# VectorE's program moved to a block border, and the first piece of wo loaded in eight parts by partitions, in a gated mix of cached attention and a feed-forward block

## The chip, the cores and the metric

The kernel runs on one core of a Trainium2 chip. The metric is device time in microseconds (us) of one execution, the median of several runs; lower is better. A core has the engines PE (TensorE: matrix products, with its weight loads as PEld), DVE (VectorE), ACT (ScalarE), POOL (GpSimd) and SP (SyncE, which here only issues DMA transfers), and 16 DMA engines that carry out the transfers between the chip's memory (HBM) and the core's memory (SBUF, 128 partitions, each a row of bytes). [...] The engines run independently and wait for each other on semaphores.

## What is computed

One token is decoded. Two branches, attention over a cache and a gated feed-forward block, are mixed by a gate:

```python
def _A_ref(x, k_cache, v_cache, wq, wo):      # Hq 32, Hkv 8, Sk 32768, Dh 128, D 512
    q = (x @ wq).reshape(B, Sq, Hq, Dh).transpose(0, 2, 1, 3)
    k = jnp.repeat(k_cache, 4, axis=1)
    v = jnp.repeat(v_cache, 4, axis=1)
    scores = jnp.einsum("bhqd,bhkd->bhqk", q, k) * (Dh ** -0.5)
    o = jnp.einsum("bhqk,bhkd->bhqd", _softmax(scores), v)
    return o.transpose(0, 2, 1, 3).reshape(B, Sq, Hq * Dh) @ wo

def _B_ref(x, w1, w3, w2):                    # F 1792
    return (_silu(x @ w1) * (x @ w3)) @ w2

g = _sigmoid((x * gate_w).sum(-1, keepdims=True))
return g * a + (1 - g) * b
```

All is float32. Keys and values are 8 heads x 32768 positions x 128 each, 134 MB apiece; wq and wo are 8.4 MB each, and w1, w3 and w2 are 3.7 MB each.

## The kernel before

The kernel is written as a list of operations for each engine (class `Program`, L24 to L115). `pr.add` records an operation with the names of what it reads and writes, and works out which semaphores it must wait for; `emit` writes each engine's list in the order in which it was recorded. So the order in the source is the order on each engine. `load` (L195) records a DMA issue on SP for a tile and takes one of nine semaphores in turn; `over` names tiles whose readers must be done first. TensorE's loops over the key units and value units are hardware loops (L701, L707); the other engines' lists are unrolled, with about 250 instructions on VectorE.

SBUF holds two buffers, `big_a` and `big_b`, each of 128 partitions x 64 KB. The keys come in 16 units and the values in 16 units, each 128 x 64 KB (8.4 MB), into one or the other buffer. A unit of keys is set aside in part by ScalarE, transposed by VectorE in blocks (L366), and multiplied with the queries by TensorE (L350). After four units come the softmax (L400 to L424) and, lagging by four units, the values' products (L451). So one unit is in the transfer queues behind the other nearly all the time, and SP issues the next as soon as its buffer's last reader is done.

At the end stand: four last units of values (`load_unit`, L589), `w2` (L604), and then `wo` (L607 to L610) into `big_a`, as `wo_t` with 32 slices of 512 numbers to a partition. It is loaded in six pieces of 16, 7, 4, 2, 2 and 1 slices (`parts`), all with 128 rows: the piece of 16 slices has 32 KB a partition. Each piece may be issued once the products of the unit that lay in `big_a` are done. TensorE multiplies with the first three pieces in `wide` (L626, its matmuls at L630), one call to a piece, each waiting for that piece's load; VectorE adds the sum to `acc` (L652), and `ff_down` (L657, L661) multiplies with the last three pieces as they come in. A copy (L673) and two stores of two rows each (SP and ScalarE, L504) end the kernel. `tile_critical` at L156 opens the part that is written by hand; ahead of it lies the opening barrier of all engines.

Of the kernel before, what the change touches and what calls it, by code (L numbers as in the profile page):

```python
# [13 lines left out]
P = 128  # L14
# [104 lines left out]
def kernel(  # L119
# [13 lines left out]
    nc = tc.nc  # L133
# [18 lines left out]
    FJ = F // 4  # L152
    assert DH == P and D == 4 * P and REP == 4 and HKV == 8 and F == FR * P and S == 4 * P * NB

    critical = ctx.enter_context(ExitStack())
    critical.enter_context(tc.tile_critical(sync_engine=mybir.EngineType.Activation, no_gpsimd_drain=True))  # L156
    pr = Program(nc, tc.alloc_semaphore)
# [12 lines left out]
    wo_t = big[0].rearrange("p (k e) -> p k e", k=32)  # L170
# [15 lines left out]
    otp = kt[1][:, 0:1024].rearrange("p (k c) -> p k c", c=32)  # L186
# [8 lines left out]
    def load(dst, src, writes, over=()):  # L195
        lanes[0] += 1
        lane = f"load{lanes[0] % 9}"
        return pr.add(
            "SP", lambda: nc.sync.dma_start(dst, src), writes=writes, over=[*over, lane], inc=lane, by=16, also=lane,  # L199
        )  # L200
# [81 lines left out]
    for c in range(NC):  # L282
        def part(c=c):
# [18 lines left out]
         reads=["gate0"], writes=["gate1"])  # L302
# [39 lines left out]
    def window(t, z):  # L342
        return act(
            lambda: A.copy(winc, win[:, t // 4, :, 16 - 16 * z:48 - 16 * z]),  # L344
            reads=[("win", t // 4, r) for r in range(4)], writes=["winc"], credit="windows",
        )
# [162 lines left out]
    first = window(0, 0)  # L509
    for t in range(NH):  # L510
# [9 lines left out]
        if t + 1 < NH:  # L520
            load_keys(t + 1)
            first = window(t + 1, 0)
# [83 lines left out]
        values(7, 0, z, region(0, z), f"A{z}")  # L606
    wod = wo.rearrange("(p k) e -> p k e", k=32)  # L607
    parts = ((0, 16), (16, 23), (23, 27), (27, 29), (29, 31), (31, 32))
    for a, b in parts:
        load(wo_t[:, a:b, :], wod[:, a:b, :], [("wo", a)], over=["A0", "A1"])  # L610


# [13 lines left out]
    def wide(i, ws, **kw):  # L626
        def go():
            for j, (w, t) in enumerate(ws):
                r = 32 * (j % 4)
                ins = T.matmul(pa[r:r + 32, :], w, t, start=(i == 0 and j < 4), stop=(final[j % 4] == (i, j)))  # L630
            return ins
        pe(go, writes=["f0"], **kw)


    def down(ks):
# [9 lines left out]
        reads=[("each", 0), ("each", 1), "otp"], writes=["lay"])  # L645
# [2 lines left out]
    down(range(3, FR))  # L648
    laid = ["otp", "lay"]
    for i, (a, b) in enumerate(parts[:3]):  # L650
        wide(i, [(otp[:, k, :], wo_t[:, k, :]) for k in range(a, b)], reads=[*laid, ("wo", a)])
    dve(lambda: V.tensor_add(acc, acc, pa), reads=["acc", "f0"], writes=["acc"])  # L652


# [27 lines left out]
    a, b, c, d = flips  # L682
# [67 lines left out]
```

## Time and profile before

| | |
|---|---|
| time, median of 3 runs | 693.98 us (693.81 to 694.11) |
| span of the profiled execution | 692.4 us |
| the profiled execution's own time beside its span | not given apart; the median lies 1.6 us above the span |
| mean granted TensorE clock | 0.790 |
| bytes read from HBM | 296.23 MB, 428 GB/s over the span |
| DMA queue q1 (SP's loads) | 6052 packets, 99.1% of 16 engines' span |
| packets of kind "instruction" | q8: 5 with 0.08 MB; q14: 3 with 0.02 MB |
| last load of wo issued, and its landing | 653.5 us, 688.5 us |

The page cuts the span into slices and gives the busy share of each engine, and for the DMA engines the mean share of the 16 and what they moved. "Instruction" packets carry program code to the engines; all other packets here are data. The windows view gives, for a stretch of time, the busy time and instructions of PE, PEld, DVE, ACT and POOL in this order, and then TensorE's clock, the DMA share and GB/s. The issue of a load stands on the SP queue (SPq); its landing is told by the semaphore that it raises.

### The profile page before, as it was taken

Reading aid. Unit: us, or ns where it says so; the run is one execution under the profiler, and the core shown is the slowest. Engines: PE = TensorE matmul, PEld = TensorE weight load, DVE = VectorE, ACT = ScalarE, POOL = GpSimd, SP = SyncE. Lnnn points to the kernel's source line nnn. Section 1 sums busy time; section 2 is a strip of 40 time slices with the busy share of each in tenths; the row PEclk is TensorE's granted clock in tenths of the full one; section 3 lists DMA queues with packets and bytes.
Section 4 is the critical chain, followed back from the end, with each engine's and each line's share of the span. In section 5 each row is a group of like instructions: output and inputs, shape, how many; then the busy total and the mean of one; then the engine's idle time right before and its main releaser. Section 6 shows DMA issues by size and latency. Waiting matters only on the chain. (4 is left out here: it accounts for less than half of the span.)

```text
span 692.4 us, 5704 instructions
## 1 busy us (share of the span) xinstructions
PE 402.8 (58%) x2430; PEld 94.6 (14%) x2430; DVE 368.4 (53%) x229; ACT 134.6 (19%) x113; POOL 8.1 (1%) x34
## 2 busy tenths in 40 slices
PE   1537777566474656557484645666573646744575
PEld 0101111201010110201010101201010102211121
DVE  0049999394735637493726537593826546700026
ACT  0143223232303130220303131210303131100000
POOL 4000000000000000000000000000000000000000
PEclk9969999958667676977786777778586777776689
DMA  9999999999999999999999999999999999999996
GB/s 386 455 428 424 424 424 436 448 443 424 428 428 428 435 454 432 424 432 428 432 454 435 424 428 428 432 435 451 432 424 428 428 435 454 435 421 424 433 421 284
DMA packets 6068, 296.34 MB, mean 428 GB/s; under 512 B 678, under 2 KB 682, under 8 KB 1068
## 3 DMA queue, kind: packets, MB, share of 16 engines
q1 hardware_dynamic: 6052, 296.23, 99.1%
q8 instruction: 5, 0.08, 0.0%
q14 instruction: 3, 0.02, 0.0%
q10 hardware_dynamic: 8, 0.01, 0.0%
HBM read 296.23 MB, written 0.00 MB: 428 GB/s over the span
## 5 line engine op out<-in xcount | busy, mean ns | idle before, releaser
L366 DVE STREAM_TRANSPOSE aside<-big_a 128x2048 f32<-128x2048 f32 x41 | 94.3, 2300 | 166.9 <-DMA big_a<-in_A_k_cache_dram 166.9
L350 PE MATMUL ps<-aside,winc 128*32 128x512 f32 x512 | 96.0, 830 | 142.4 <-PEq L688 141.5
L350 PE MATMUL ps<-kt,winc 128*32 128x512 f32 x512 | 96.2, 832 | 61.2 <-PEq L688 61.2
L451 PE MATMUL ps<-big_b,pv 128*32 128x512 f32 x768 | 96.1, 657 | 17.5 <-PEq L688 17.5
L338 ACT COPY aside<-big_a 128x6144 f32<-128x6144 f32 x14 | 74.4, 5313 | 151.8 <-DMA big_a<-in_A_k_cache_dram 151.8
L366 DVE STREAM_TRANSPOSE kt<-aside 128x2048 f32<-128x2048 f32 x32 | 73.4, 2293 | 17.2 <-PE ps L350 17.2
L366 DVE STREAM_TRANSPOSE kt<-big_a 128x2048 f32<-128x2048 f32 x28 | 63.5, 2269 | 0.0
L379 ACT COPY sb<-ps 128x512 f32<-128x512 f32 x16 | 17.1, 1069 | 156.8 <-PE ps L350 156.8
L350 PEld LDWEIGHTS ps<-aside,winc 128*32 128x32 f32 x512 | 13.4, 125 | 215.7 <-issue 215.7
L451 PEld LDWEIGHTS ps<-big_b,pv 128*32 128x32 f32 x768 | 27.7, 120 | 88.1 <-issue 88.1
L366 DVE STREAM_TRANSPOSE aside<-aside 128x2048 f32<-128x2048 f32 x16 | 36.3, 2269 | 0.0
L583 DVE TENSOR_TENSOR sb<-ps,own_b 128x512 f32<-128x512 f32 x2 | 1.4, 691 | 60.8 <-PE ps L574 60.8
L350 PEld LDWEIGHTS ps<-kt,winc 128*32 128x32 f32 x512 | 13.3, 123 | 143.8 <-issue 143.8
L574 PE MATMUL ps<-big_b,probs 128*32 128x512 f32 x128 | 18.0, 726 | 18.8 <-DMA big_b<-in_A_v_cache_dram 18.8
L344 ACT COPY winc<-win 128x128 f32<-128x128 f32 x32 | 9.8, 306 | 78.7 <-PE ps L350 78.7
L574 PE MATMUL ps<-big_a,probs 128*32 128x512 f32 x128 | 17.3, 703 | 10.1 <-DMA big_a<-in_A_v_cache_dram 10.1
L614 PE MATMUL ps<-win,ones 128*128 128x512 f32 x42 | 22.7, 635 | 0.0
L366 DVE STREAM_TRANSPOSE aside<-big_b 128x2048 f32<-128x2048 f32 x7 | 16.0, 2291 | 11.4 <-DMA big_b<-in_A_k_cache_dram 11.4
L262 PE MATMUL ps<-acc 128*128 128x512 f32 x34 | 20.0, 670 | 2.5 <-POOL acc L219 1.6
L400 DVE TENSOR_REDUCE mt<-turned 128x8 f32<-128x2048 f32 x4 | 9.2, 2291 | 22.6 <-PE turned L389 22.6
L424 DVE TENSOR_REDUCE sums<-probs 128x8 f32<-128x2048 f32 x4 | 15.2, 3801 | 2.1 <-ACT probs L417 2.1
L288 PE MATMUL turned<-big_a,xp 128*32 128x512 f32 x64 | 8.5, 691 | 12.1 <-DMA big_a<-in_A_wq_dram 12.1
(93 smaller groups left out, 186.6 us busy)
## 6 DMA issues: line engine op xcount, KB each, us to landing
big_b<-in_B_w_dram SPq DMA_DIRECT2D x2, 3584.0 KB, 20.8
big_a<-in_A_wo_dram SPq DMA_DIRECT2D x1, 4096.0 KB, 27.6
aside<-in_B_w_dram SPq DMA_DIRECT2D x1, 3584.0 KB, 37.4
big_a<-in_A_wo_dram SPq DMA_DIRECT2D x1, 1792.0 KB, 31.5
big_a<-in_A_wo_dram SPq DMA_DIRECT2D x1, 1024.0 KB, 33.5
big_a<-in_A_wo_dram SPq DMA_DIRECT2D x2, 512.0 KB, 34.7
big_a<-in_A_wo_dram SPq DMA_DIRECT2D x1, 256.0 KB, 35.2
big_a<-in_A_k_cache_dram SPq DMA_DIRECT2D x14, 26.3
```

The costliest lines, as they stand in the source:

```text
L262: return T.matmul(ps_s, acc[:, 0:P], acc, start=True, stop=False, skip_group_check=True)
L288: ins = T.matmul(pf[b][32 * j:32 * j + 32, :], xp[:, c, :], t[:, o:o + REP * DH], start=(c == 0), stop=(c == NC - 1),)
L338: act(lambda: A.copy(spare, src[:, :, 32:128]), reads=[key], writes=["wo"])
L344: lambda: A.copy(winc, win[:, t // 4, :, 16 - 16 * z:48 - 16 * z]),
L350: ins = T.matmul(ps_s[32 * g:32 * g + 32, :], winc[:, c, :], kt[c % 2][:, 512 * g:512 * g + 512], start=False, stop=False, skip_group_chec ...
L366: k = dve(lambda d=dst, s=src: V.transpose(d, s), reads=[key], writes=[f"kt{c % 2}"], over=["kt0"] * (t >= LAG and (z, c) == (1, 1)), cred ...
L379: lambda: A.copy(sb[:, :, :, t % 4], ps_s.rearrange("p (n i) -> p n i", i=32)),
L400: dve(lambda: V.tensor_reduce(mt[:, 0:8], turned.rearrange("p (n q) -> p q n", q=8), axis=AX.X, op=ALU.max), reads=banks, writes=["mt"])
L424: dve(lambda: V.tensor_reduce(sums[:, 8 * w:8 * w + 8].rearrange("p (u q) -> p u q", u=2), probs[:, :, 0:1024].rearrange("p u (n q) -> p u ...
L451: ins = T.matmul(ps_o[32 * t:32 * t + 32, :], pv[:, o:o + 32], big[1][:, n * P:(n + 4) * P], start=((z, g) == (0, 0)), stop=((z, g) == (1, ...
L574: ins = T.matmul(ps_o[32 * t:32 * t + 32, :], prob[u][:, o:o + 32], vt[:, n * P:(n + 4) * P], start=((e, z, g) == (0, 0, 0)), stop=((e, z, ...
L614: return T.matmul(bank[:, 0:n], ones, win.rearrange("p w c n -> p (w c n)")[:, 0:n], start=True, stop=True)
```

## The change

The first edit is one instruction for VectorE alone, ahead of the hand-written part: `addr_align(128, offset=0, max_nops=0)` has the loader put what follows at the next multiple of 128 instructions in VectorE's program, and has it jumped to, not padded with no-ops.

The second is the first piece of wo, the one with 16 slices. It was one load of 128 rows with 32 KB each. It becomes: one load of the rows 112 to 127 with 13 of the 16 slices (26 KB a row), six loads of the last three slices of these rows (6 KB a row), three rows at a time and the last with one, and one load of the rows 0 to 111 with all 16 slices. The eight loads raise one common semaphore, `first`, and the first call of `wide` waits for all of them. The other five pieces are as before.

```diff
+    nc.vector.addr_align(128, offset=0, max_nops=0)
     critical = ctx.enter_context(ExitStack())
...
     parts = ((0, 16), (16, 23), (23, 27), (27, 29), (29, 31), (31, 32))
-    for a, b in parts:
+    top_rows, split = 112, 13
+    pieces = [(top_rows, P, 0, split)]
+    pieces += [(p, min(p + 3, P), split, 16) for p in range(top_rows, P, 3)]
+    pieces += [(0, top_rows, 0, 16)]
+    first = [("wo", 0, i) for i in range(len(pieces))]
+    for key, (p, q, a, b) in zip(first, pieces):
+        pr.add("SP", lambda p=p, q=q, a=a, b=b: nc.sync.dma_start(wo_t[p:q, a:b, :], wod[p:q, a:b, :]),
+               writes=[key], over=["A0", "A1"], inc="first", by=16)
+    for a, b in parts[1:]:
         load(wo_t[:, a:b, :], wod[:, a:b, :], [("wo", a)], over=["A0", "A1"])
...
     for i, (a, b) in enumerate(parts[:3]):
-        wide(i, [(otp[:, k, :], wo_t[:, k, :]) for k in range(a, b)], reads=[*laid, ("wo", a)])
+        landed_keys = [("wo", a)] if i else first
+        wide(i, [(otp[:, k, :], wo_t[:, k, :]) for k in range(a, b)], reads=[*laid, *landed_keys])
```

On SP, behind the last unit of values, the loads of w2 (`in_B_w`) and wo stood so before (destination, source, and the rows and numbers to a row of each):

```order
L199 DMA aside<-in_B_w_dram 128x7168
L199 DMA big_a<-in_A_wo_dram 128x8192
L199 DMA big_a<-in_A_wo_dram 128x3584
L199 DMA big_a<-in_A_wo_dram 128x2048
L199 DMA big_a<-in_A_wo_dram 128x1024 x2
L199 DMA big_a<-in_A_wo_dram 128x512
```

And so they stand now (the lines of the changed kernel are one or ten higher):

```order
L200 DMA aside<-in_B_w_dram 128x7168
L616 DMA big_a<-in_A_wo_dram 16x6656
L616 DMA big_a<-in_A_wo_dram 3x1536 x5
L616 DMA big_a<-in_A_wo_dram 1x1536
L616 DMA big_a<-in_A_wo_dram 112x8192
L200 DMA big_a<-in_A_wo_dram 128x3584
L200 DMA big_a<-in_A_wo_dram 128x2048
L200 DMA big_a<-in_A_wo_dram 128x1024 x2
L200 DMA big_a<-in_A_wo_dram 128x512
```

The load of 128 rows with 8192 numbers each has become eight; all others keep their place and shape.

At the start of VectorE's list, the branch that waits for the opening barrier was followed at once by the branch that waits for ScalarE's opening of the hand-written part:

```order
L745 UNCONDITIONAL_BRANCH [waits barrier_Pool_Activation_PE_DVE_SP_release]
L745 UNCONDITIONAL_BRANCH [waits Activation_sequencer_49]
L279 COPY xp<-ps 128x4 [waits PE]
L298 TENSOR_REDUCE gsm<-tmp 1x1 [waits POOL]
L309 STREAM_TRANSPOSE aside<-probs 128x512 [waits ACT]
```

Now the alignment stands between the two (the row "ISA"):

```order
L755 UNCONDITIONAL_BRANCH [waits barrier_Pool_Activation_PE_DVE_SP_release]
L155 ISA
L755 UNCONDITIONAL_BRANCH [waits Activation_sequencer_49]
L280 COPY xp<-ps 128x4 [waits PE]
L299 TENSOR_REDUCE gsm<-tmp 1x1 [waits POOL]
L310 STREAM_TRANSPOSE aside<-probs 128x512 [waits ACT]
```

No other engine has it, and VectorE's own operations keep their order.

## The prediction

> **What bounds the kernel now.** I read the page's slices first, then the queues, the chain of waits, and last the end of the span in narrow windows.
>
> ```profile
> span 692.4 us, 5704 instructions
> PE 402.8 (58%) x2430; PEld 94.6 (14%) x2430; DVE 368.4 (53%) x229; ACT 134.6 (19%) x113; POOL 8.1 (1%) x34
> DMA  9999999999999999999999999999999999999996
> DMA packets 6068, 296.34 MB, mean 428 GB/s; under 512 B 678, under 2 KB 682, under 8 KB 1068
> q1 hardware_dynamic: 6052, 296.23, 99.1%
> q8 instruction: 5, 0.08, 0.0%
> q14 instruction: 3, 0.02, 0.0%
> ```
>
> No engine is busy for 60% of the span, but the 16 DMA engines are at nine tenths in every slice but the last: q1, SP's loads, keeps them busy for 99.1%. So the kernel is its bytes. An engine at work moves 428 / (16 x 0.991) = 27.0 GB/s, that is 27.0 KB (of 1000 bytes) a microsecond. Two things may shift an end that is already full: bytes dealt unevenly to the 16 engines, and a lower rate. The last two rows matter for the first: eight packets of q8 and q14 fetch program code (0.08 / 5 = 16 KB and 0.02 / 3 = 8 KB each) and go through the same engines.
>
> The row of packets also tells how many engines a load uses. The kernel's 42 loads of 128 rows, if each closes on 16 engines with a small packet, make 672 of the 678 packets under 512 B; the two loads of one row (x, gate_w) add 2 if they close on one engine each, and the two stores of two rows add 4 if they close on two each. 672 + 2 + 4 = 678. So 128 rows go to 16 engines, two rows to two and one row to one; I take three rows to go to three, and 16 and 112 rows to sixteen.
>
> The chain that ended last:
>
> ```profile
> 651.67 0.33 SPq L199
> ...
> 653.46 35.07 DMA big_a<-in_A_wo_dram
> 688.53 0.04 issue
> 688.58 1.10 PE turned L661 x24
> 689.68 0.02 issue
> 689.70 0.29 DVE winc L673
> ```
>
> The last loads of wo set the end; behind them stand only the last products, one copy and the store. What those loads gain or lose, the kernel gains or loses. The end in windows (time, engines, then clock, DMA share, GB/s):
>
> ```profile
> 686.00:686.50 0.50, 0.42 (x4) 0.16 (x8) 0.00 (x0) 0.00 (x0) 0.00 (x0) 1.00 0.97 373
> 686.50:687.00 0.50, 0.50 (x8) 0.00 (x0) 0.00 (x0) 0.00 (x0) 0.00 (x0) 1.00 0.60 238
> 687.00:687.50 0.50, 0.30 (x11) 0.15 (x11) 0.28 (x1) 0.00 (x0) 0.00 (x0) 1.00 0.36 147
> 687.50:688.00 0.50, 0.50 (x20) 0.26 (x16) 0.40 (x1) 0.00 (x0) 0.00 (x0) 1.00 0.38 147
> 688.00:688.40 0.40, 0.39 (x8) 0.12 (x8) 0.00 (x0) 0.00 (x0) 0.00 (x0) 1.00 0.24 92
> 688.40:688.80 0.40, 0.22 (x8) 0.23 (x12) 0.00 (x0) 0.00 (x0) 0.00 (x0) 1.00 0.06 20
> ```
>
> At 27.0 GB/s an engine, 147 GB/s are between five and six engines: the others are through by 687.0, and the last ends at about 688.7 (20 GB/s over 0.40 us is 8 KB, 0.3 us of one engine). Some six engines are up to 1.7 us late, which fits the eight fetches. What is moved after 686.5 is 119 + 74 + 74 + 37 + 8 = 312 KB; sixteen engines would need 312 / 432 = 0.7 us, so a perfect balance ends at 687.2. **No re-dealing can gain more than 1.5 us of 694.**
>
> **The change, part by part.** (1) The block border. Two of VectorE's blocks are fetched during the loads; the later one, in the list of DMA queues cut to 497 to 499 us:
>
> ```profile
> DMA packets 14, 0.86 MB, mean 430 GB/s; under 512 B 0, under 2 KB 0, under 8 KB 0
> q14 instruction: 1, 0.01, 1.0%
> ```
>
> and by windows VectorE (the third pair of numbers) starts some 128 instructions between this fetch and one at 119.2:
>
> ```profile
> 119.20:497.50 378.30, 224.61 (x1326) 49.69 (x1326) 217.80 (x129) 82.62 (x62) 0.00 (x0) 0.75 1.00 433
> ```
>
> 129 overlap the window and one was running when it opened, so a block is 128 instructions of 8 KB. VectorE has 229 and a few waits, under 256: begun on a border it crosses one border in the run and not two, and the jump to the first block falls ahead of the loads' data. So one fetch less, 8 KB / 27.0 = 0.30 us at the least on one engine. It moves the end only if that engine is the last, and then no further than the next: I take 0.2 (0 to 0.3). A jump that has to wait for its block is hidden, since VectorE first works here:
>
> ```profile
> 11.18 0.17 DVE L279 COPY xp<-ps 128x4 f32<-128x4 f32 x1 [11.18 <-PE ps L273]
> ```
>
> Ten microseconds of cover; nobody else waits for VectorE at the opening. If the jump also stalled the other engines, that stall would be added whole.
>
> (2) The dealing. Before, an engine moves 8 rows of 32,768 B in the first piece, 9.71 us. After, it moves one row of 26,624 B and seven of 32,768 B: 9.48 us, 0.23 less. Three engines also get five rows of 6,144 B, together 0.91 us more than before, and one of them the last row too, 1.14 more. If these three are on time now, they end at 687.0 + 1.14 = 688.1, and the late ones at 688.7 - 0.23, less 0.2 by (1): 688.25. So 0.45 us are gained, if rates stay.
>
> (3) SP issues 13 loads in place of 6.
>
> ```profile
> 651.67 2.70 SPq L199 DMA_DIRECT2D big_a<-in_A_wo_dram x6
> big_a<-in_A_wo_dram SPq DMA_DIRECT2D x1, 4096.0 KB, 27.6
> ```
>
> 2.70 / 6 = 0.45 us each, 3.15 us for seven more. The piece lands 27.6 us after its issue and needs 9.7 itself, so 17.9 us of older loads hide this; without them it would be 3.15 us. TensorE's wait for the piece becomes one wait for its eight loads; behind it stand all later products of wo, and for these VectorE's last two instructions and the store. The piece ends ahead of the next five pieces in every case, and the next one bound it already:
>
> ```profile
> 679.39 3.64 PE L630 MATMUL turned<-big_a,kt 128*32 128x512 f32 x32 [3.17 <-DMA big_a<-in_A_wo_dram]
> 683.59 1.92 PE L630 MATMUL turned<-big_a,kt 128*32 128x512 f32 x14 [0.56 <-DMA big_a<-in_A_wo_dram]
> ```
>
> Cost nothing, unless that load is later than the following ones.
>
> (4) The rate. Here the trace is silent: it holds no large load of fewer than 128 rows. With 128 rows, sixteen engines fill sixteen lots of eight partitions, one lot each. Its 27.0 GB/s may be what an engine can send, or what a lot of eight partitions can take; the rows agree with both. If it is the lot, then the new loads are slow, since several engines write into one lot.
> - Sixteen rows of 26,624 B (426 KB): 0.99 us if they lie in 16 lots, 426 / (2 x 27.0) = 7.9 us if in two. Which rows share a lot no row shows; I take four lots, near the geometric middle of 2 and 16 (5.7) on the side of neighbours sharing: 3.9 us, so +2.9 (0 to +6.9).
> - 112 rows, 3,670 KB. Fourteen lots at full rate need 9.7 us against 7 x 1.21 = 8.5, +1.2; with each lot shared by two engines all the time +8.5. I take the middle, +4.85.
> - Three neighbouring rows: 18.4 KB into one lot is 0.68 us, five times 3.4, and 0.2 for the last row, in place of 1.4: +2.2 on the three engines.
>
> These three are the last then: 687.0 + 1.14 + 2.9 + 4.85 + 2.2 = 698.1, against 688.7: **+9.4 us**. At the low ends it is (687.0 + 1.14 + 0 + 1.2 + 0) = 689.3, +0.6; at the high ends of the first two terms +17.
>
> [...]
>
> [...]
>
> **The rivals.**
> A, my forecast: the lot limits. For it: full rate is only ever seen with one engine to a lot, and the new loads are the first to break that. Against it: no row shows sharing at all. 693.98 + 9.4 = 703.4 us; 697 to 708 within it. It decides as soon as the shared loads lose more than the 0.45 that dealing gains.
> B, not slower: the engine limits, and the dealing works as in (2): 693.98 - 0.45 = 693.5 us (693.2 to 693.9). For it: the late engines of the last windows, which it serves.
> C: as B, but one of the three engines that get more is a late one: 688.5 + 1.14 = 689.6, +0.9 at most, some 694.5 us. Six late of sixteen, but one whole engine would have to be hit.
> D: as B, but a three-row load runs on one engine: 15 x 6,144 and 6,144 B more make 98 KB less the 6 KB, 3.4 us on one engine, 690.4, +1.7: 695.7 us. Against it: two rows went to two.
> E: the fetches delay more than their bytes, and the dealing evens all: at most -1.5, 692.5 us.
>
> **How the numbers follow.** The sum is made on the profiled execution: its span is 692.4 us, and 1.6 us lie around it, up to the median of 693.98; I leave those alone. A differs from B by one unknown that the rows leave even; I give A a little more than half, since it is the only reading under which the even layout of before matters: A 0.51, B 0.34, C 0.09, D 0.04, E 0.02. About 0.2% (1.4 us) is what a measurement of this kernel can tell from no change: slower is A and D, 0.55; the same is B and C, 0.43; faster is E, 0.02. The predicted time is A's, 703.4. The range has to hold B as well: 693.2 to 708, which leaves out A's far end (some 0.08) and E; A alone spans 697 to 708.
>
> **What would show it.** A: in the windows from 667 to 690 us DMA moves well under 400 GB/s with its packets still open (share near 1), the first wide product (679.39 now) starts 6 us or more later, and the last product of wo moves by about 9 us. Were the rate still near 430 there, the lot doesn't limit, and A falls whole. B: the tail under 200 GB/s, 1.7 us long now, is 1.2 to 1.4 long. (1): two q14 packets of 8 KB in the run in place of three, and VectorE's one fetch some 128 instructions from its start, near 370 us. (3): 13 issues of 0.4 us each from 651.7, and the next piece's landing no later than the dealing says. My prediction is wrong if engines that share eight partitions keep 27 GB/s each; its size is wrong if the 112 rows are dealt so that they seldom meet.

## The result, and the profile after

The changed kernel takes 704.6 us (median of 5 runs, 704.2 to 707.06) against 693.98 us (5 runs, 693.81 to 694.11): 1.0164 times the time of before, 95% interval 1.0152 to 1.0175. It is 10.6 us slower. The profiled execution of after took 704.2 us, with a span of 702.5 us; as before, 1.6 to 1.7 us lie around the span. Runs in a slower state (784.55 us at a TensorE clock of 0.684 and 1837.39 us at 1.0 of the kernel before, 716.39 us at 0.657 of one kernel below) are left out of all times below.

The page of after, in the lines that answer to those of before:

```profile
span 702.5 us, 5712 instructions
DMA packets 6116, 296.34 MB, mean 422 GB/s; under 512 B 710, under 2 KB 714, under 8 KB 1116
q1 hardware_dynamic: 6100, 296.23, 99.2%
q14 instruction: 3, 0.02, 0.0%
```

The bytes are the same and the DMA engines are as busy as before, 99.2%; only the rate is lower, 422 GB/s in place of 428. Packets under 512 B have grown from 678 to 710. The new loads explain the 32 if a load closes, with one small packet on each, on as many engines as the prediction took: 16 + 5 x 3 + 1 + 16, less the 16 of the old load.

The windows view of both kernels over the end (time, busy time of the engines, TensorE's clock, DMA share, GB/s). Before:

```profile
653.00:667.00 14.00, 5.93 (x40) 1.51 (x44) 0.00 (x0) 0.00 (x0) 0.00 (x0) 0.63 0.99 425
667.00:671.00 4.00, 3.84 (x30) 0.90 (x22) 1.10 (x2) 0.00 (x0) 0.00 (x0) 1.00 1.03 441
671.00:676.00 5.00, 4.34 (x10) 1.82 (x10) 4.89 (x6) 0.00 (x0) 0.00 (x0) 1.00 1.00 426
676.00:682.00 6.00, 2.83 (x27) 1.01 (x30) 5.75 (x9) 0.00 (x0) 0.00 (x0) 1.00 0.92 392
682.00:686.00 4.00, 2.94 (x26) 0.52 (x18) 2.83 (x4) 0.00 (x0) 0.00 (x0) 1.00 0.98 401
```

After:

```profile
653.00:667.00 14.00, 6.42 (x36) 1.62 (x40) 0.00 (x0) 0.00 (x0) 0.00 (x0) 0.63 1.00 413
667.00:671.00 4.00, 4.00 (x34) 1.02 (x26) 0.64 (x1) 0.00 (x0) 0.00 (x0) 1.00 1.18 163
671.00:676.00 5.00, 4.18 (x10) 1.82 (x10) 3.93 (x6) 0.00 (x0) 0.00 (x0) 1.00 0.82 157
676.00:682.00 6.00, 0.72 (x2) 0.00 (x0) 5.79 (x7) 0.00 (x0) 0.00 (x0) 0.80 1.11 311
682.00:686.00 4.00, 0.00 (x0) 0.00 (x0) 3.82 (x6) 0.00 (x0) 0.00 (x0) 0.50 0.83 191
686.00:690.00 4.00, 0.41 (x4) 0.23 (x8) 0.43 (x1) 0.00 (x0) 0.00 (x0) 0.50 0.90 267
690.00:697.00 7.00, 7.00 (x54) 1.97 (x46) 0.00 (x0) 0.00 (x0) 0.00 (x0) 0.77 0.99 408
698.00:699.00 1.00, 0.69 (x24) 0.46 (x24) 0.34 (x1) 0.00 (x0) 0.00 (x0) 1.00 0.29 111
```

Up to 667 us, while the old kind of load is in the queues, after runs near before's rate (413 GB/s against 425). Then, from the first of the new loads on, the DMA share stays near 1 (0.82 to 1.18 in single windows, 0.99 over the 19 us), but up to 686 us the engines move 157 to 311 GB/s where before moved 392 to 441. They have packets open and bring in less. From 690 on, with the whole-width pieces, the rate is back at 408. The chain that ended last, of after:

```profile
652.73 36.73 DMA big_a<-in_A_wo_dram
689.46 0.14 issue
689.60 8.04 PE turned L639 x51
697.65 0.70 DVE acc L662
698.35 0.04 issue
698.40 1.40 PE turned L671 x32
```

The first wide product starts at 689.60 us, 10.2 us later than before (679.39). Its operations then stand in the chain, since TensorE had waited 12.9 us and works at half clock at first (0.50 in the windows up to 690); but the transfers too last into the window from 698 to 699. The landing at 688.53 us in the chain of before is that of the last load of wo but one. The last itself, of 256 KB, was issued at 653.9 us and landed 35.2 us later, at 689.1; in after it was issued at 655.0 and landed 44.3 us later, at 699.3, ten microseconds after that of before. One run further down separates the transfers from TensorE's products.

### The profile page after: what moved, and what is told of

The parts are those of the page before. It is cut to its first block, busy times and chain, and to the rows that moved or that the text cites. A ratio compares the mean times of both kernels' runs of the same rounds, so it can differ in the third digit from the quotient of the medians.

```text
span 702.5 us, 5712 instructions
## 1 busy us (share of the span) xinstructions
PE 388.9 (55%) x2430; PEld 93.7 (13%) x2430; DVE 368.7 (52%) x229; ACT 134.7 (19%) x113; POOL 8.1 (1%) x34
## 3 DMA queue, kind: packets, MB, share of 16 engines
q1 hardware_dynamic: 6100, 296.23, 99.2%
## 5 line engine op out<-in xcount | busy, mean ns | idle before, releaser
L351 PE MATMUL ps<-aside,winc 128*32 128x512 f32 x512 | 90.2, 782 | 152.2 <-PEq L698 151.4
L351 PE MATMUL ps<-kt,winc 128*32 128x512 f32 x512 | 90.2, 783 | 66.2 <-PEq L698 66.2
L452 PE MATMUL ps<-big_b,pv 128*32 128x512 f32 x768 | 92.2, 635 | 17.5 <-PEq L698 17.5
L367 DVE STREAM_TRANSPOSE aside<-big_b 128x2048 f32<-128x2048 f32 x7 | 16.1, 2298 | 11.0 <-DMA big_b<-in_A_k_cache_dram 10.6
## 6 DMA issues: line engine op xcount, KB each, us to landing
big_a<-in_A_wo_dram SPq DMA_DIRECT2D x1, 256.0 KB, 44.3
```

Of the source, the lines that this page charges most:

```text
L351: ins = T.matmul(ps_s[32 * g:32 * g + 32, :], winc[:, c, :], kt[c % 2][:, 512 * g:512 * g + 512], start=False, stop=False, skip_group_chec ...
L367: k = dve(lambda d=dst, s=src: V.transpose(d, s), reads=[key], writes=[f"kt{c % 2}"], over=["kt0"] * (t >= LAG and (z, c) == (1, 1)), cred ...
L452: ins = T.matmul(ps_o[32 * t:32 * t + 32, :], pv[:, o:o + 32], big[1][:, n * P:(n + 4) * P], start=((z, g) == (0, 0)), stop=((z, g) == (1, ...
```

## The experiments

The theory is that of the prediction's case A: a lot (a group of eight partitions, as the prediction assumed; which partitions is part of the question) takes 27 GB/s, and engines that write into the same lot share it. The rivals: the number of loads and their issue; the uneven bytes and small loads on three engines; the block border; TensorE's late products; the source in HBM. Each time stands beside runs of the kernel before on the same chip, whose medians were 693.8 to 694.0 us.

**Loads alone.** A kernel that only loads rows of wo, each load when the last has landed:

```diff
+    for n, (p, q, step, k) in enumerate(stages):
+        pr.add("SP", lambda p=p, q=q, s=step, k=k: nc.sync.dma_start(wo_t[p:q:s, 0:k, :], wod[p:q:s, 0:k, :]),
+               writes=["big"], inc=f"stage{n}", by=16)
```

> No attention at all: fourteen loads of rows of wo, each issued when the one before has landed, so that each is seen alone. It leaves out the whole computation; the output is zeros. [...] If the engine limits: every packet at 27 GB/s whatever the rows.

The windows view of this kernel, one window around each of eight loads (time, POOL's busy time, clock, DMA share, GB/s): 128 rows, rows 112 to 127, sixteen rows 8 apart, rows 0 to 111, rows 0 to 31, rows 0 to 63, three neighbouring rows of 6 KB, four rows 32 apart. Each window holds one load whole, with some idle time at its ends.

```profile
1.80:12.70 10.90, 0.00 (x0) 1.00 0.95 385
13.70:17.60 3.90, 0.00 (x0) 1.00 0.72 109
20.00:22.70 2.70, 0.00 (x0) 1.00 0.65 158
24.10:39.70 15.60, 0.00 (x0) 1.00 0.93 235
41.10:47.10 6.00, 0.00 (x0) 1.00 0.80 175
48.80:59.80 11.00, 0.00 (x0) 1.00 0.91 191
61.20:61.80 0.60, 0.00 (x0) 1.00 0.11 31
73.40:75.00 1.60, 0.00 (x0) 1.00 0.20 67
```

The loads of 16 rows and more go to sixteen engines, as the count of small packets has it: the page of this kernel has 145 under 512 B, which is 7 x 16 for the loads of 16 rows and more, 32 for the 32 rows of the smaller loads and one for the store. But the sixteen neighbouring rows come in at 109 GB/s, which is 4 x 27, and 32 and 64 rows at less than half of the 385 of 128 rows (175 and 191). The load of 112 rows, which has seven eighths of the bytes, takes 15.6 us in place of 10.9. The small loads came in faster than one lot's 27 GB/s: four neighbouring rows of 26 KB took less than 2.8 us and not 3.9, and three rows of 6 KB less than 0.6 us and not the 0.68 of the prediction. So the shorter rows share less than the theory says, and the next kernel takes longer ones. Here near partitions always went with near rows of wo, so the source could be what is shared.

**Source and destination apart.** The same with rows of 64 KB, and the partitions chosen apart from the rows of wo:

```diff
+    one, near, four_apart = (0, 1, 1), (0, 4, 1), (0, 16, 4)
+    far, low, spread = (0, 128, 32), (0, 16, 1), (0, 128, 8)
...
+        pr.add("SP", lambda d=d, s=s: nc.sync.dma_start(wo_t[d[0]:d[1]:d[2]], wod[s[0]:s[1]:s[2]]),
```

> Again loads of rows of wo alone, one after the other, zeros as output and nothing else computed; now rows of 65,536 B (2.42 us alone at 27 GB/s), and the partitions that are written and the rows of wo that are read are chosen apart: four near, 4 apart or 32 apart; sixteen neighbours or 8 apart; 64 neighbours or every second. If the destination's partitions are what is shared: four neighbouring partitions take 5.5 to 9.7 us whether the rows of wo are near or 32 apart, and partitions 32 or 4 apart take about 2.6 us, also with neighbouring rows of wo; sixteen neighbouring partitions 8.9 to 9.7 us with either source, sixteen that lie 8 apart 5 to 6 us with either. If the source in HBM is what is shared, it goes by the rows of wo and not by the partitions. [...]

Its windows, one load in each: partitions 0 to 3 with near rows of wo; the same partitions with rows 32 apart; partitions 32 apart with near rows; partitions 4 apart with near rows; partitions 0 and 32; partitions 0 and 64; partitions 0 to 15 with near rows and with rows 8 apart; sixteen partitions 8 apart with near rows; then 64 neighbouring partitions with near rows and with every second row; last the 64 even partitions, with near rows.

```profile
6.20:15.60 9.40, 0.00 (x0) 1.00 0.23 28
17.60:26.80 9.20, 0.00 (x0) 1.00 0.22 28
29.10:34.10 5.00, 0.00 (x0) 1.00 0.22 52
36.10:39.80 3.70, 0.00 (x0) 1.00 0.19 71
51.60:56.60 5.00, 0.00 (x0) 1.00 0.11 26
65.70:68.90 3.20, 0.00 (x0) 1.00 0.11 41
69.90:79.70 9.80, 0.00 (x0) 1.00 0.89 107
81.60:91.40 9.80, 0.00 (x0) 1.00 0.88 107
93.60:99.60 6.00, 0.00 (x0) 1.00 0.80 175
108.80:129.90 21.10, 0.00 (x0) 1.00 0.95 199
131.70:152.70 21.00, 0.00 (x0) 1.00 0.96 200
154.50:165.70 11.20, 0.00 (x0) 1.00 0.92 374
```

Four partitions side by side take one engine's rate together, 28 GB/s, and it makes no difference which rows of wo they hold; with the same rows of wo but 4 apart they move 71 in a window that has its idle ends too. Four partitions 32 apart took 5.0 us and not the expected 2.6 (52 GB/s, the rate of two). That fits the pairs: partitions 0 and 32 share (26 GB/s), 0 and 64 do not (41 over 3.2 us, with the start in it). Partitions 0 to 15 have 107 GB/s with either source, and 8 apart 175. 64 neighbours have 199 GB/s, about half of the 385 of 128 rows, and 64 even partitions nearly all of it, 374. So the destination decides, and the source falls. A lot is not eight neighbours: four neighbours share, and so do two partitions 32 apart. Which partitions make up a whole lot, and whether they are eight, these loads don't show. The shorter rows of the kernel ahead of this one share only in part (last section).

**The piece in eight loads by slices.** As many loads as in the change, one common semaphore, but all rows in each:

```diff
-    pieces = [(top_rows, P, 0, split)]
...
+    pieces = [(0, P, 2 * i, 2 * i + 2) for i in range(8)]
```

> The first piece again in eight loads with the one common semaphore, and the alignment, but divided by slices: each load has all 128 rows and two slices. If partitions limit, nothing is shared and the time is that of the kernel before, 693.5 to 694.3 us. If it is the number of loads, their issue on SP or the common semaphore that costs, the time stays near the changed kernel's 704.6 us.

694.28 us (10 runs), 1.0005 times before, 0.9995 to 1.0014. The number of loads, their issue and the semaphore cost nothing that can be measured.

**Two loads, without the small ones.**

```diff
-    top_rows, split = 112, 13
...
+    top_rows = 112
+    pieces = [(top_rows, P, 0, 16), (0, top_rows, 0, 16)]
```

> The six small loads are left away: rows 112 to 127 and rows 0 to 111 are loaded whole, with 16 slices each, in two loads; every engine moves as many bytes as before the change. If partitions limit, most of the loss stays: 702 to 704.5 us. If the loss comes from the extra bytes and loads on three engines, it goes: 693.5 to 694.5 us.

706.89 us (705.7 to 708.1, 3 runs), ratio 1.0187 (1.0165 to 1.0209). The loss is there without any extra byte on three engines. At 13.0 us it is 2.4 us above the range given. The sixteen rows are longer here, 32 KB in place of 26, and that takes only part of it (at the 109 GB/s measured alone, 0.9 us); where the rest comes from stays open.

**The same bytes on each engine, but fewer of them shared.**

```diff
-    pieces = [(top_rows, P, 0, split)]
+    pieces = [(0, P, 0, split)]
...
-    pieces += [(0, top_rows, 0, 16)]
+    pieces += [(0, top_rows, split, 16)]
```

> Every engine moves the same bytes as in the changed kernel, and the six small loads are the same, but 13 of the 16 slices come in one load of all 128 rows, and only the last three slices of rows 0 to 111 come in a load of 112 rows. If partitions limit: no sixteen-row load (about -3 us), and the loss of the 112-row load is cut to 6/32; with the small loads' some 2 us the time is 695 to 698 us. If the loss hangs on how many bytes each engine carries or on the small loads alone, it stays at 704 to 705 us.

696.42 us (5 runs), ratio 1.0037 (1.0023 to 1.0052). In its windows the rate holds up to the small loads, and falls only with them and with the short load of 112 rows:

```profile
667.00:671.00 4.00, 3.42 (x26) 0.78 (x18) 1.52 (x2) 0.00 (x0) 0.00 (x0) 1.00 1.00 425
676.00:682.00 6.00, 0.05 (x4) 0.08 (x8) 5.75 (x8) 0.00 (x0) 0.00 (x0) 0.66 0.97 241
682.00:686.00 4.00, 4.00 (x28) 1.17 (x32) 2.38 (x4) 0.00 (x0) 0.00 (x0) 0.65 0.98 413
```

With each engine's bytes as in the change and all its small loads, 2.6 us are lost and not 10.6. How many bytes an engine gets is not what costs.

**The piece in eight loads of sixteen rows**, once neighbours and once every eighth row, with the same engines, packets and bytes in both:

```diff
+    pieces = [(p, p + 16, 0, 16) for p in range(0, P, 16)]
```

```diff
+    pieces = [(p, P, 0, 16) for p in range(8)]
...
+        pr.add("SP", lambda p=p, q=q, a=a, b=b: nc.sync.dma_start(wo_t[p:q:8, a:b, :], wod[p:q:8, a:b, :]),
```

The first is called blocks below, the second combs.

> The changed kernel with its first piece in eight loads of 16 neighbouring rows, 32 KB each: every engine moves one row of each load, 256 KB as before the change, in eight packets as before. If engines that write neighbouring partitions share their rate, the first piece takes 25 to 32 us in place of 9.7: 709 to 716 us. If engines alone limit, 694 us.

> As the kernel with eight loads of 16 neighbouring rows, but each load takes every eighth row: same engines, bytes, packets, loads and semaphore, other rows together. If neighbouring partitions share: two engines meet in a lot and not four, so the loss is less than half of the other's, 699 to 703 us. If it is the number or size of the loads: the same as the other kernel.

Blocks: 715.4 us (713.43 to 719.77), ratio 1.033 (1.0282 to 1.0378). Combs: 705.77 us (705.46 to 707.2), ratio 1.0169 (1.0149 to 1.0189). The order is as expected, but combs lost 12.0 us against the other's 21.6, a little over half, and more than the range given. The range was too low by its own theory: two engines to a lot all the time double the piece's 9.7 us, which is 9.7 us of loss and not 5 to 9. The window from 682 to 686 of blocks, then of combs:

```profile
682.00:686.00 4.00, 0.00 (x0) 0.00 (x0) 3.82 (x6) 0.00 (x0) 0.00 (x0) 0.50 0.90 156
```

```profile
682.00:686.00 4.00, 0.00 (x0) 0.00 (x0) 3.62 (x5) 0.00 (x0) 0.00 (x0) 0.50 0.95 197
```

**Even and odd rows.** Two loads of 64 rows:

```diff
+    pieces = [(p, P, 0, 16) for p in range(2)]
...
+        pr.add("SP", lambda p=p, q=q, a=a, b=b: nc.sync.dma_start(wo_t[p:q:2, a:b, :], wod[p:q:2, a:b, :]),
```

> The changed kernel with its first piece in two loads, of the even rows and of the odd rows, 64 rows of 32 KB each. Alone, 64 rows that lie 2 apart went at the full 27 GB/s an engine, 64 neighbours at half. If lots of partitions are all that costs, the piece is as fast as in one load: 693.6 to 694.4 us. If loads of fewer than 128 rows cost something of their own inside the kernel, where the engines are not in step, the time is above 695 us.

693.74 us (11 runs), ratio 1.0001 (0.9992 to 1.001). Loads of half the rows cost nothing that can be measured when the rows lie two apart.

**The border alone, and the loads alone.**

```diff
+    nc.vector.addr_align(128, offset=0, max_nops=0)
```

The first of the two kernels has this line alone, added to the kernel before; the second is the changed kernel without it. A third run is the changed kernel once more.

> The block border alone, on the kernel before. One fetch of 8 KB less among the loads' data: 0.1 to 0.4 us less than before, 693.6 to 693.9 us, hardly above what can be measured; VectorE's fetches at the start and near 303 us as in the changed kernel. If the jump to the border stalled the start, the first load would start later than 2.0 us and the time would be above 694.2 us.

> The eight loads alone, without the block border. If partitions limit, the whole loss is here: 704 to 707 us, as the changed kernel. If the border had a share in the loss, the time would be at least 1 us below the changed kernel's.

> The changed kernel once more, for its spread beside the others on one chip: 704 to 707.5 us by any theory. If the block border helped or hurt by more than 1 us, it would stand apart from the 706.5 to 709 us of the kernel with the eight loads alone.

The border alone: 693.7 us (11 runs) beside 693.97, ratio 0.9997 (0.9988 to 1.0006): no difference that can be measured, though in its profile the last wo landing in the chain is at 688.02 and not 688.53 us. VectorE's fetches were expected at the start and near 303 us, and both q14 packets came there (2.0 and 303.1 us). The loads alone: 707.16 us (706.45 to 708.95), 1.0199 (1.0184 to 1.0215). The changed kernel again: 707.48 us (704.76 to 709.04), 1.0202 (1.0182 to 1.0222). The border has no share in the loss that these runs could show.

**TensorE kept at work** in its long wait:

```diff
-    for _ in range(4):
+    for _ in range(18):
         idle_product(512)
```

> The changed kernel with 14 more idle products on TensorE ahead of the first wide product, so that its 13 us of waiting there is filled. If the later product chain on a slowed clock has a share in the loss (the changed kernel's runs spread from 704.2 to 707.1 us), the time falls to 703.5 to 704.2 us and the spread is gone. If the transfers alone set the end, the time and the spread stay as they are.

707.38 us (705.55 to 709.14), ratio 1.0202 (1.0187 to 1.0218). The clock shows that the idle products do what they should: from 686 to 690 us it is 1.00 here, and was 0.50 in the changed kernel. The window, and the chain of this kernel:

```profile
686.00:690.00 4.00, 2.67 (x7) 0.88 (x5) 0.00 (x0) 0.00 (x0) 0.00 (x0) 1.00 0.93 252
```

```profile
654.47 44.79 DMA big_a<-in_A_wo_dram
699.25 0.04 issue
699.30 1.11 PE turned L671 x24
```

The wide products are off the chain, and the transfers end it, as before the change. In the profile of the changed kernel run again, without the idle products, they end it too, at the same time:

```profile
654.49 44.72 DMA big_a<-in_A_wo_dram
699.22 0.04 issue
```

The time stays as it is without the idle products (707.16 us, 706.45 to 708.95, for the eight loads alone on the same chip), and the spread is no smaller, so TensorE's slowed products run beside transfers that end as late. In some profiles they do end a little later: with the eight loads alone 1.5 us after the last load has landed, in the run again 0.5. So up to 1 us of a single run may be theirs.

## Why the prediction was right

**What bounds the kernel.** The step held: the end moved with the last loads of wo. They land ten microseconds later, and the span is 10.1 us longer.

**The rate, term (4).** It was the whole result. The prediction could not tell an engine's 27.0 GB/s from a lot's; loads with source and destination apart did: a lot's. Four partitions side by side took 28 GB/s together, whichever rows of wo they held, and four that lie 4 apart 71. The sum was 9.4 us and 10.6 were measured (13.7 when the kernel was run again on another chip).

Its terms held less well than their sum. Four lots for rows 112 to 127 fits the 109 GB/s (4 x 27) measured alone, though no row stood behind that choice. The 112 rows were put at +4.85 us, the middle between two bounds; alone the load took 15.6 us, against 10.9 x 7 / 8 = 9.5 for its share of 128 rows, so +6.1, which would add 1.2 us to the sum. The "fourteen lots" of this term took eight neighbours for a lot, which partitions 0 and 32 refute (26 GB/s together). No run shows that count, nor the low bound of +1.2 that was worked out from it; the 15.6 us lie between the two bounds, 9.7 and 17.0.

The three-row loads were put at 0.68 us each and +2.2 in all. Alone, one was over within 0.6 us, idle ends included; in a narrower window that still holds its 18.4 KB it is 0.45 us:

```profile
61.30:61.75 0.45, 0.00 (x0) 1.00 0.15 41
```

At 0.45 us, five of them and the last row cost about 1.1 us more than their 1.4 at full rate, and not 2.2. So, by the loads alone, this term was about twice too large and the one of the 112 rows too small by as much, and the two errors cancel. The kernel with 13 slices over all rows lost 2.6 us with the three-row loads and 6/32 of the 112-row bytes, which fits the prediction's terms (1.14 + 2.2 + 0.9, less the 1.7 by which the late engines are late anyway), but doesn't separate them. And the two loads without the small ones lost 13.0 us, no less than the kernels that have them. So the mechanism was right; that the sum came within 1.2 us of the measured loss is partly luck, for how its terms add up inside the kernel, where the loads overlap, was not measured.

**The dealing, term (2).** Its 0.45 us never had a chance to show. Rivals B and E, 693.5 and 692.5 us, fall with the change's 704.6; the full-width 694.28 and the even and odd 693.74 us show that it is not the dividing into several loads that costs. Rival D, one engine for a three-row load, falls with the 710 small packets, if an engine closes a load with one. Whether one of the three engines is a late one (C) stays open; its 0.9 us could not make 10.6.

**The border, term (1).** The gain was put at 0.2 us, and the runs can't tell it from nothing. But the expectation for the trace was wrong in two places. The page still counts three q14 packets and not two. One, at 136 us, was there before (138) and is neither of the two between which the prediction counted VectorE's instructions. Those two, at 119.2 and 497.5 us before, moved with VectorE's program, to 2.0 and 303 us. The one of the jump, at 2.0 us, falls just as the loads begin, and not ahead of them. And the other comes at 303 us, not near 370, after some 104 of VectorE's instructions and not 128:

```profile
2.10:303.00 300.90, 170.32 (x1016) 40.60 (x1015) 177.39 (x104) 77.53 (x69) 6.11 (x26) 0.83 1.00 433
```

(The third pair is VectorE's.) So the block of 128 instructions stays the prediction's estimate, from the 129 between 119.2 and 497.5 us; why the packet comes after 104, the runs don't show.

**The issue and the waits, term (3).** The issues were hidden, as eight loads over all rows show; the eight of the change took 2.61 us, not 8 x 0.45. But "cost nothing" for TensorE's wait had lost its cover: the first wide product came so late that its chain ended together with the transfers. The kernel with more idle products was no faster, so this added nothing to the median that could be measured.

## What to carry to other kernels

Before dealing a load differently, ask which partitions its engines write at the same moment, and not only how many bytes each engine has: here sixteen engines into sixteen neighbouring partitions had the rate of four (109 GB/s, 4 x 27), while 64 partitions two apart had nearly that of 128 (374 GB/s against 385). A balance that may gain half a microsecond should be tried with loads that span all partitions: eight such loads took 694.28 us, the eight of the change 704.6. Read the DMA share beside the GB/s: here the share stayed near 1 while the rate fell to 157 GB/s, and the share alone would have looked like full work.

## What the runs showed that was not expected

Short rows partly escape the sharing: four neighbouring rows of 26 KB came in at 38 GB/s in a window with both idle ends, more than one lot's rate, while rows of 64 KB came in at 28. Four rows 32 apart moved 67 GB/s with 26 KB and 52 with 64 KB, and three neighbours of 6 KB 41. Why, no run tests. The window of the first, in the kernel that only loads:

```profile
64.50:67.30 2.80, 0.00 (x0) 1.00 0.21 38
```

The kernels whose loads share lots vary more from run to run (704.76 to 709.04 us for the changed kernel on one chip) than before does (693.57 to 694.59 over 14 runs on another chip). Why, no run tests.
